# Attention and two expert layers on one core: another order of the first transfers, other places for the steps of the heads, and two of three blocks of the first chunk among the last heads

## The chip, the core and the metric

The kernel runs on one core of a Trainium2 chip. Its engines work side by side, each through its own queue in order: TensorE (PE; its weight loads are PEld), VectorE (DVE), ScalarE (ACT), GpSimd (POOL) and SyncE (SP), which issues all the DMAs. The metric is the device time of one execution in microseconds.

## The reference

```python
q_assign = argmax(q_n @ c_n)            # per head, 16 normalised centroids
k_assign = argmax(k_n @ c_n)
mask = q_assign[:, :, :, None] == k_assign[:, :, None, :]
scores = where(mask, scale * q @ k.T, -1e9); attn = softmax(scores) @ v   # 2 x 8 heads, 768 x 64
x = attn.transpose(0, 2, 1, 3).reshape(1536, 512)
p = domain_probs / (domain_probs.sum(-1) + 1e-9)
out = sum over 4 experts e of p[:, e] * (relu(x @ w1[e]) @ w2[e])     # 512 -> 1024 -> 512
h = out @ w_in; result = maximum(0.01 * h, h) @ w_out                 # 512 -> 2048 -> 512
```

## The kernel before

The sixteen (batch, head) pairs are heads t = 0 to 15; two make a pair `pr`. For each head the kernel needs a stack of q and k halves (`qka`, `qkb`), made from `pair` by three DMAs (`restack`), and two small DMAs that add the one-hot cluster rows (`restack_oh`). Pieces of a head:

- `M(t,j)`, j = 0 to 5: scores of 128 rows on PE, their row maximum by DVE (L416). `mrow(t)`: PE transposes the six maxima, ACT copies them, a DMA writes them into `qka`; E of that head needs it.
- `E(t,s)`: scores on PE (L447, L448), exponential on ACT into one of three `p` buffers. `P(t,s)`: `phi` and the rest `plo`, in float16. POOL makes `plo`, but in heads 14 and 15 DVE does.
- `V(t,j)`: 18 small products (L473 to L475) that read `phi` and `plo` of all six s. `norm(t)`: division on DVE. `X(pr)`: PE transposes a finished pair, ACT and DVE split it into `xhi` and `xlo`, the input of the first expert layer.
- For a coming pair: `prep_load` of q, k, v; `prep_T` (transposes of q, k); `prep_simT`, `sims_argmax`, three argmax pieces and `prep_ohT` (the cluster rows); `prep_vmax`, `prep_vall`, `prep_vscale` and `prep_v` (v scaled and split).

PE results go through three double banks `big()` in turn, V through two single ones. All steps stand in one list (`at(when, ...)`), sorted by a hand-written place: `E(t,s)` has place 6t + s, and constants such as `M_AT`, `V_AT`, `MROW_AT` and `RESTACK_AT` give the others relative to a head or a pair. Each engine takes its part of the steps in that order, SP its DMAs too. So a DMA that must wait holds up all DMAs behind it.

At the start the SP order is: q, k of pairs 0 and 1; restack(0); v of pair 0; restack(1); v of pair 1; the small `dp`; the one-hot rows of head 1; restack(2), restack(3); q, k of pair 2; the one-hot rows of heads 2 and 3; q, k of pair 3.

`open_early` (place 78.5) closes the pool `prep` and loads the first weights `w1raw` and the probabilities `pb`; `split_early` (84.5) splits these weights (ACT, POOL) and loads the next ones into the same `w1raw`.

The expert layers run in 16 and then 8 chunks of 256 hidden columns: hidden products for three blocks u of 512 tokens, an epilogue (DVE `g`, ACT `hhi`, POOL `hlo`), then twelve output tiles. Of chunk 0, block u = 0 (24 products, L637) is put among the last steps: 12 before the last head's V, 6 behind them, 6 behind X(7); its epilogue `h_finish` is one DVE instruction over two banks (L656). The pools `main` and `psum_a` are then closed, `ffn` and `psum_f` opened over the same memory, and blocks 1 and 2 follow (L872). `input_sums` are 18 steps for the later seven-product chunks, spread by `quota` over chunks 0 and 1.

Of the kernel before, what the change touches and what calls it, by code (L numbers as in the profile page):

```python
# [8 lines left out]
F32 = mybir.dt.float32  # L9
# [5 lines left out]
ALU = mybir.AluOpType  # L15
# [3 lines left out]
PHI_AT = 0.97  # L19
PHI_ON_VECTOR = ((0, 2, 5), (3,))  # L20
PLO_ON_VECTOR = ((), ())
M_AT = ((0.72, 1.85, 2.02, 3.21, 4.53, 5.24), (0.67, 1.71, 2.17, 2.76, 4.15, 5.08))
V_AT = ((1.8, 2.31, 3.68, 4.42, 5.11, 5.44), (1.09, 2.97, 3.59, 4.57, 5.82, 5.87))
NORM_AT = (6.53, 6.37)
PREP_V_AT = (2.42, 2.77)
MROW_AT = (-0.08, 1.32)
X_AT = 4.26
VMAX_AT = 3.85
VSCALE_AT = 7.41
T_AT = (3.21, 3.57)  # L30
SIMT_AT = 5.56
SIMS_AT = 6.98
ARGMAX_AT = (1.05, 2.1, 2.22)
OHT_AT = 3.04
RESTACK_AT = (0.42, 1.63)


M0_AT = (-6.63, -3.55, -2.57, -2.19, -1.41, -1.01)
# [8 lines left out]
PHI_FIRST = ((1, 2), (3, 5))  # L47
WARM = (7, 2, 6)
WARM_AT = (4.39,)

BIG = float(2 ** 60)
HEAD_ROOM = 64.0
# [7 lines left out]
def attention_moe_kernel(  # L60
# [13 lines left out]
    nc = tc.nc  # L74
    B, H, S, D = q.shape
# [7 lines left out]
    J = S // 128  # L83
# [22 lines left out]
    def big():  # L106
        pool, tag = bigs[turns[0] % len(bigs)]
        turns[0] += 1
        return pool.tile([128, 1024], F32, tag=tag, name=tag)
# [25 lines left out]
    def h_set(pool):  # L135
        n = len(hbuf)
        hbuf.append([pool.tile([128, FCH // 128, NT], F32R, name=f"h{x}{n}") for x in ("hi", "lo")])
        gbuf.append(pool.tile([128, FCH // 128, 512], F32, name=f"g{n}"))
        pbuf.append(pool.tile([128, 1, NT], F32, name=f"pb{n}"))
# [47 lines left out]
    def split_halves(hi, lo, src):  # L187

        nc.scalar.activation(out=hi, in_=src, func=AF.Copy)  # L189
        n = src.shape[1] // 2  # L190
        for x in (slice(0, n), slice(n, 2 * n)):
            nc.gpsimd.tensor_tensor(out=lo[:, x], in0=src[:, x], in1=hi.bitcast(F32)[:, x], op=ALU.subtract)  # L192

    def weights_split(part):
        hi, lo = (w1s, w2s)[part][0]
        split_halves(hi, lo, raw12[part])

    def weights_sums():

# [372 lines left out]
    prep_T(0, 0)  # L572
    prep_T(0, 1)
    restack(0)
    prep_load(0, "v")
    restack(1)
    prep_load(1, "v")
    dp = prep.tile([128, NTILE, E], F32, name="dp")
    nc.sync.dma_start(
        out=dp.rearrange("p (b j) e -> p b (j e)", b=B),  # L580
# [40 lines left out]
    NF = FCH // 128  # L621
    h_ps = {}

    def h_products(c, u, n0, n1):

        if n0 == 0:
            h_ps[c, u] = big()
        pv = h_ps[c, u].rearrange("p (f t) -> p f t", f=NF)
        whi, wlo = w1s[0]
        us = slice(u * 512, (u + 1) * 512)  # L630
        n = 0
        for f in range(NF):
            fs = slice(f * 128, (f + 1) * 128)
            for kc in range(KC):
                for i, (w, x) in enumerate(((whi, xhi), (whi, xlo), (wlo, xhi))):
                    if n0 <= n < n1:
                        nc.tensor.matmul(  # L637
                            pv[:, f, :], lhsT=w[:, kc, fs], rhs=x[:, kc, us],
                            start=kc + i == 0, stop=kc == KC - 1 and i == 2,
                        )  # L640
                    n += 1
# [21 lines left out]
            nc.vector.tensor_tensor(out=g, in0=src, in1=g, op=ALU.max)  # L663
        split(hi, lo, g, nc.gpsimd)

    def h_finish(c, u):
        h_split(c, u, 0, h_ps.pop((c, u)).rearrange("p (f t) -> p f t", f=NF))

    NMM = 3 * NF * KC

    def open_early():
        st_prep.close()
        early = ctx.enter_context(tc.tile_pool(name="early", bufs=1, side="right"))
        w1_set(early)
        raw12.append(early.tile([128, KC, FCH], F32, name="w1raw"))
        h_set(early)
        weights_load(0, 0)
        probs_load(0)

    def split_early():  # L680
        weights_split(0)
# [5 lines left out]
    def at(when, fn, *args):  # L687
        line.append((when, len(line), fn, args))

    for t in range(NH):  # L690
        o = J * t
        par = t % 2
        for s in range(J):
            at(o + s, emit_E, t, s)
            if t < NH - 2:
                at(o + s + PHI_AT, emit_P, t, s, s in (PHI_ON_VECTOR[par] if t > 1 else PHI_FIRST[t]), s in PLO_ON_VECTOR[par])
            else:
                at(o + s + PHI_AT, emit_P, t, s, s % 2 == 0, True)
        for j in range(J):
            if t > 1:  # L700
                at(o - 2 * J + M_AT[par][j] if t > 3 else (M2_AT, M3_AT)[t - 2][j], emit_M, t, j)
            at(o + J + V_AT[par][j], emit_V, t, j)
        at(o + J + NORM_AT[par], emit_norm, t)
        at(o + PREP_V_AT[par] if t > 0 else EARLY["v0"], prep_v, t)
        if t > 1:
            at(o - J + MROW_AT[par] if t > 3 else EARLY[f"mrow{t}"], emit_mrow, t)
# [34 lines left out]
    at(EARLY["ohT0"] + 0.01, restack_oh, 1)  # L741
    for t in (2, 3):
        at(EARLY["restack"], restack, t)
    for nm in "qk":
        at(EARLY["restack"] + 0.01, prep_load, 2, nm)
    for t in (2, 3):
        at(EARLY["ohT1"] + 0.01, restack_oh, t)
    at(EARLY["vmax"], prep_vmax, 0)
# [4 lines left out]
    for when in WARM_AT:  # L753
        at(when, warm, 1)
    at(J * (NH - 3) + 0.5, open_early)
    at(J * (NH - 2) + 0.5, split_early)

    end = J * NH + V_AT[(NH - 1) % 2][0]
    at(end - 0.01, h_products, 0, 0, 0, NMM // 2)
    end = J * NH + NORM_AT[(NH - 1) % 2]  # L760
    at(end + 0.01, h_products, 0, 0, NMM // 2, 3 * NMM // 4)
    at(J * (NH + 1) + X_AT + 0.01, h_products, 0, 0, 3 * NMM // 4, NMM)
    at(J * (NH + 1) + X_AT + 0.02, h_finish, 0, 0)
    for _, _, fn, args in sorted(line, key=lambda x: x[:2]):
        fn(*args)
    st_main.close()
# [2 lines left out]
    ffn = ctx.enter_context(tc.tile_pool(name="ffn", bufs=1))  # L769
    psum_f = ctx.enter_context(tc.tile_pool(name="psum_f", bufs=1, space=bass.MemoryType.PSUM))  # L770
    w2_set(ffn)
    raw12.append(ffn.tile([128, FCH // 128, DM], F32, name="w2raw"))
    gbuf.append(ffn.tile([128, FCH // 128, 512], F32, name="g1"))
    pbuf.append(ffn.tile([128, 1, NT], F32, name="pb1"))
    acc = ffn.tile([128, NTILE * DM], F32, name="acc")
# [192 lines left out]
    def is_wide(c):  # L968
        return wide and chunks[c][3] is None

    weights_load(0, 1)
    probs_load(1)
    turns[1] = 0
    PLAIN = (0, 1, N1, N1 + 1)
# [1 line left out]
    for c in range(NCH):  # L976

        steps = []
        if c + 1 < NCH and is_wide(c + 1):
            steps += weights_narrow(c + 1, 0)  # L980
            if c + 2 < NCH:
                steps.append(lambda: weights_load(c + 2, 0))
        if c + 1 < NCH and not is_wide(c + 1):
            steps.append(lambda: weights_load(c + 1, 1))
        if c in PLAIN:
            weights_split(1)
            if c == 0:
                sums_left = input_sums(False)
                quota = [5, 5, 5, 5]
            n = quota.pop(0)  # L990
            slots = steps + sums_left[:n]
            sums_left = sums_left[n:]
            blocks = [(u, f) for u in range(1 if c == 0 else 0, NU) for f in range(NF)]
            for n, (u, f) in enumerate(blocks):
                if c > 0:
                    ps = bank(BANKS[u][f])
                    plain(c, u, f, ps)
                elif f == 0:
                    both_ps = [bank(BANKS[u][f]) for f in range(NF)]
                    for k in range(KC):  # L1000
                        for g in range(NF):
                            plain(c, u, g, both_ps[g], [k])
                if c == 0:
                    ps = both_ps[f]
                h_split(c, u, f, ps)
                for _ in range(-(-len(slots) // (len(blocks) - n))):
                    step = slots.pop(0)
                    if step:
                        step()
        else:  # L1010
            emit_seven(c, steps)

        steps, later = [], []
        if c in PLAIN:
            n = quota.pop(0)
            later, sums_left = sums_left[:n], sums_left[n:]
        if c + 1 < NCH:
            if is_wide(c + 1):
                later += weights_narrow(c + 1, 1)
                if c + 2 < NCH:  # L1020
                    later.append(lambda: weights_load(c + 2, 1))
            steps.append(lambda: weights_split(0))
            if c + 1 not in PLAIN:
                steps += weights_sums()
            if c + 2 < NCH and not is_wide(c + 2):
                steps.append(lambda: weights_load(c + 2, 0))
        if c == N1 - 5 and wide:
            steps += [lambda: weights_load(N1, 0), lambda: weights_load(N1, 1)]
        if c < N1 and c % (FE // FCH) == 0 and 0 < chunks[c][3] < E - 1:
            steps.append(lambda: probs_load(chunks[c][3] + 1))  # L1030
        steps = [x for pair in zip_longest(steps, later) for x in pair if x]
        for i in range(NTILE):
            if c == N1 - 1 and i == NTILE - 1:
                sums_left = input_sums(True)
                quota = [3, 2, 4, 4]
                sums_left.pop(0)()
            (emit_y1 if c < N1 else emit_y2)(c, i)
            for _ in range(-(-len(steps) // (NTILE - i))):
                steps.pop(0)()
# [32 lines left out]
```

## Time and profile before

| | us |
|---|---|
| three runs, median | 1045.18 (1044.88 to 1045.35) |
| profiled execution | 1047.64 |
| its span, first to last instruction | 1045.9 |
| PE busy in the span | 1012.0 (97%) |
| DVE, POOL, ACT busy | 674.9, 602.2, 400.9 |
| mean granted TensorE clock | 0.992 |

PE is busy in nearly all of the span; a queue of matmuls counts as busy, at full clock or at half. What the chip does otherwise with its time shows where PE waits or where its clock is down.

### The profile page before, as it was taken

The numbers are of one execution on the slowest core, as the hardware profiler recorded it, in microseconds if no ns is written. First come the engines' busy times: TensorE is split into PE (matmuls) and PEld (weight loads), VectorE is DVE, ScalarE is ACT, GpSimd is POOL, SyncE is SP. The second block draws the span as 40 slices with busy tenths as digits, with TensorE's granted clock in tenths as the row PEclk, the third lists the DMA queues.
The fourth block names the chain that finished last, engine by engine and source line by source line (L and its number), as shares of the span: only waits on it lengthen the run. The fifth ranks groups of instructions, "written<-read, shape, count | busy, mean of one in ns | idle before, by whom it ended". The sixth has DMA issues, their size and how long they took to land.

```text
span 1045.9 us, 15196 instructions
## 1 busy us (share of the span) xinstructions
PE 1012.0 (97%) x6064; PEld 824.5 (79%) x6064; DVE 674.9 (65%) x964; ACT 400.9 (38%) x554; POOL 602.2 (58%) x468
## 2 busy tenths in 40 slices
PE   7689999999999999999999999999999999999998
PEld 5578888878788888888888888888877888888886
DVE  7698888887754454444544445544587678777765
ACT  3467777775321222212122222222245433344331
POOL 4267777781645566545665455654577565665553
PEclk9899999999999999999999999999999999999999
DMA  7854666540310110210111103101111221122103
GB/s 174 171 111 109 137 146 145 115 102 21 72 40 21 41 41 24 68 36 25 40 52 40 41 21 121 41 21 41 40 41 41 81 81 43 45 74 81 41 1 121
DMA packets 59535, 70.74 MB, mean 68 GB/s; under 512 B 25060, under 2 KB 42088, under 8 KB 59464
## 3 DMA queue, kind: packets, MB, share of 16 engines
q1 hardware_dynamic: 59464, 69.77, 25.4%
q8 instruction: 48, 0.79, 0.3%
q14 instruction: 23, 0.19, 0.1%
HBM read 46.19 MB, written 3.17 MB: 47 GB/s over the span
## 4 chain that ended last, share of the span: by engine, by line
PE 70%; DVE 3%; ACT 1%; issue 0%; POOL 0%; DVEq 0%; POOLq 0%
PE z L862 18%; PE z L872 15%; PE z L939 8%; PE z L938 8%; PE z L937 8%; PE z L955 4%; PE z L957 4%; PE z L956 4%; ACT xhi L119 0%; DVE xlo L120 0%; DVE acc L944 0%; DVE g L663 0%; POOL hlo L120 0%; DVE w2raw L173 0%; DVE w2raw L182 0%
## 5 line engine op out<-in xcount | busy, mean ns | idle before, releaser
L120 POOL TENSOR_TENSOR hlo<-g,hhi 128x512 fp32r<-128x512 f32 (+1 forms) x143 | 198.5, 1396 | 293.7 <-ACT hhi L119 292.3
L944 DVE TENSOR_TENSOR acc<-z,acc 128x512 f32<-128x512 f32 x180 | 124.0, 690 | 101.5 <-PE z L939 101.4
L461 POOL TENSOR_TENSOR plo<-p,phi 128x768 f16<-128x768 f32 x84 | 138.1, 1656 | 85.2 <-ACT phi L460 47.0
L119 ACT ACTIVATE hhi<-g 128x512 fp32r<-128x512 f32 (+1 forms) x143 | 89.5, 635 | 189.7 <-DVE g L656 143.9
L939 PE MATMUL z<-hlo,w2hi 128*128 128x512 f32 x384 | 152.9, 398 | 0.0
L938 PE MATMUL z<-hhi,w2lo 128*128 128x512 f32 x384 | 151.6, 395 | 0.0
L937 PE MATMUL z<-hhi,w2hi 128*128 128x512 f32 x384 | 150.9, 393 | 0.4 <-DVE acc L944 0.4
L656 DVE SCALAR_TENSOR_TENSOR g<-z,pb 128x512 f32<-128x512 f32 x80 | 55.0, 688 | 92.5 <-PE z L872 86.5
L872 PE MATMUL z<-xhi,w1hi 128*128 128x512 f32 x248 | 98.2, 396 | 1.7 <-DVE g L656 1.7
L872 PE MATMUL z<-xlo,w1hi 128*128 128x512 f32 x248 | 98.4, 397 | 0.0
L872 PE MATMUL z<-xhi,w1lo 128*128 128x512 f32 x248 | 98.2, 396 | 0.0
L416 DVE TENSOR_REDUCE m<-big 128x1 f32<-128x768 f32 x96 | 90.2, 949 | 12.1 <-PE big L412 10.8
L450 ACT ACTIVATE p<-big 128x768 f32<-128x768 f32 x96 | 77.8, 810 | 37.4 <-PE big L448 34.0
L938 PEld LDWEIGHTS z<-hhi,w2lo 128*128 128x128 f32 x384 | 72.1, 188 | 18.3
L937 PEld LDWEIGHTS z<-hhi,w2hi 128*128 128x128 f32 x384 | 72.1, 188 | 18.1 <-DVE acc L944 0.8
L939 PEld LDWEIGHTS z<-hlo,w2hi 128*128 128x128 f32 x384 | 72.1, 188 | 16.8
L955 PE MATMUL z<-w2hi,hhi 128*128 128x512 f32 x192 | 76.7, 400 | 2.2 <-DVE acc L960 2.2
L447 PE MATMUL big<-qka 128*128 128x512 f32 x192 | 73.2, 382 | 4.0 <-DMA qka<-mrow 2.1
L956 PE MATMUL z<-w2lo,hhi 128*128 128x512 f32 x192 | 76.8, 400 | 0.0
L957 PE MATMUL z<-w2hi,hlo 128*128 128x512 f32 x192 | 76.8, 400 | 0.0
L895 DVE TENSOR_TENSOR part<-z,part 128x512 f32<-128x512 f32 x60 | 41.5, 692 | 52.3 <-PE z L862 42.2
L192 POOL TENSOR_TENSOR w2lo<-w2raw,w2hi 128x512 fp32r<-128x512 f32 x48 | 61.2, 1298 | 22.9 <-ACT w2hi L189 22.9
(196 smaller groups left out, 2291.6 us busy)
## 6 DMA issues: line engine op xcount, KB each, us to landing
qkb<-pair SPq DMA_DIRECT2D x32, 384.0 KB, 6.8
w1raw<-in_moe_w_dram SPq DMA_DIRECT2D x16, 512.0 KB, 3.5
w2raw<-in_moe_w_dram SPq DMA_DIRECT2D x16, 512.0 KB, 3.6
w1raw<-in_moe_w_in_dram SPq DMA_DIRECT2D x8, 1024.0 KB, 7.1
w2raw<-in_moe_w_out_dram SPq DMA_DIRECT2D x8, 1024.0 KB, 5.0
qka<-pair SPq DMA_DIRECT2D x16, 384.0 KB, 4.0
vraw<-in_v_dram SPq DMA_DIRECT2D x16, 192.0 KB, 3.0
pb<-pe_rows SPq DMA_DIRECT2D x4, 768.0 KB, 8.0
```

Of the source, the lines that this page charges most:

```text
L120: lo_engine.tensor_tensor(out=lo, in0=src, in1=hi.bitcast(F32), op=ALU.subtract)
L416: nc.vector.tensor_reduce(out=m_t[t][:, j:j + 1], in_=ps[:, 0:S], op=ALU.max, axis=AX.X)
L461: (nc.vector if plo_on_vector else nc.gpsimd).tensor_tensor(out=plo, in0=p, in1=phi, op=ALU.subtract)
L862: nc.tensor.matmul(ps[:, 0, :], lhsT=w[i][:, k, :], rhs=x[j][:, k, :], start=first and k + i + j == 0, stop=k == 1 and i == 1, skip_group_ ...
L872: nc.tensor.matmul(ps[:, 0, :], lhsT=w[:, k, fs], rhs=x[:, k, us], start=k + i == 0, stop=k == KC - 1 and i == 2,)
L937: nc.tensor.matmul(ps, lhsT=whi[:, f, ks], rhs=hi[:, f, us], start=f == 0, stop=False)
L938: nc.tensor.matmul(ps, lhsT=wlo[:, f, ks], rhs=hi[:, f, us], start=False, stop=False)
L939: nc.tensor.matmul(ps, lhsT=whi[:, f, ks], rhs=lo[:, f, us], start=False, stop=f == NF - 1)
L944: nc.vector.tensor_tensor(out=a, in0=ps, in1=a, op=ALU.add)
L955: nc.tensor.matmul(ps, lhsT=hi[:, f, ts], rhs=whi[:, f, :], start=f == 0, stop=False)
L956: nc.tensor.matmul(ps, lhsT=hi[:, f, ts], rhs=wlo[:, f, :], start=False, stop=False)
L957: nc.tensor.matmul(ps, lhsT=lo[:, f, ts], rhs=whi[:, f, :], start=False, stop=f == NF - 1)
```

## The change

Most step places of the steady heads, the order of the first transfers, the place of the second weights' loads, and the place and epilogue of the first chunk's blocks 0 and 1 are other ones; the last two heads get V and norm places of their own. The DMAs at the start now go: restack(0), restack(1), q and k of pair 2, `dp`, one-hot rows of head 1, v of pair 0, restack(2), restack(3), v of pair 1, one-hot rows of heads 2 and 3. `w2raw` is loaded in `open_early`, behind `w1raw` and `pb`. Block 0 is finished before X(7) but for its epilogue; block 1 has six products before X(7) and eighteen behind it; the epilogues are single-bank instructions whose `g` lies in the `p` buffers. `w2lo` of chunk 0 is made by one DVE instruction in place of two on POOL.

```diff
-M_AT = ((0.72, 1.85, 2.02, 3.21, 4.53, 5.24), (0.67, 1.71, 2.17, 2.76, 4.15, 5.08))
-V_AT = ((1.8, 2.31, 3.68, 4.42, 5.11, 5.44), (1.09, 2.97, 3.59, 4.57, 5.82, 5.87))
-NORM_AT = (6.53, 6.37)
-MROW_AT = (-0.08, 1.32)
+M_AT = ((1.25, 2.08, 2.35, 3.21, 5.26, 5.79), (0.67, 1.9, 2.06, 2.76, 4.04, 5.42))
+V_AT = ((1.84, 2.15, 2.31, 3.56, 4.97, 5.13), (1.44, 2.97, 3.24, 4.31, 4.57, 5.82))
+NORM_AT = (6.53, 6.12)
+MROW_AT = (1.43, 0.25)
...
-VSCALE_AT = 7.41
+VSCALE_AT = 9.19
...
-SIMS_AT = 6.98
-ARGMAX_AT = (1.05, 2.1, 2.22)
-OHT_AT = 3.04
-RESTACK_AT = (0.42, 1.63)
+SIMS_AT = 6.7
+ARGMAX_AT = (1.36, 2.0, 2.3)
+OHT_AT = 3.0
+RESTACK_AT = (-0.21, 1.47)
...
+V_LAST = ((1.23, 2.31, 4.28, 5.08, 5.75, 5.98), (1.09, 1.44, 1.57, 4.46, 5.87, 5.87))
+NORM_LAST = (6.49, 6.57)
+PHI_LAST = ((0, 2, 4), (0, 2, 4))
+SPLIT_AT = (0.94,)
+FILL = ((0, 0, 1.07), (0, 6, 1.08), (0, 12, 6.38), (0, 18, 6.39), (1, 0, 9.94), (1, 6, 10.27), (1, 12, 10.27))
...
     restack(0)
-    prep_load(0, "v")
     restack(1)
-    prep_load(1, "v")
+    prep_load(2, "qk")
...
+    def h_finish_early(u):
+        hi, lo = [x[:, :, u * 512:(u + 1) * 512] for x in hbuf[0]]
+        pv = h_ps.pop((0, u)).rearrange("p (f t) -> p f t", f=NF)
+        for f in range(NF):
+            g = main.tile([128, S], F32, tag="p", name="p", bufs=3)[:, 0:512]
+            nc.vector.scalar_tensor_tensor(
+                out=g, in0=pv[:, f, :], scalar=0.0, in1=pbuf[0][:, 0, u * 512:(u + 1) * 512], op0=ALU.max, op1=ALU.mult,
+            )
+            split(hi[:, f, :], lo[:, f, :], g, nc.gpsimd)
...
         weights_load(0, 0)
         probs_load(0)
+        weights_load(0, 1)
...
-    for nm in "qk":
-        at(EARLY["restack"] + 0.01, prep_load, 2, nm)
+    at(EARLY["ohT0"] + 0.02, prep_load, 0, "v")
+    at(EARLY["restack"] + 0.01, prep_load, 1, "v")
...
-    at(J * (NH - 2) + 0.5, split_early)
+    at(J * (NH - 2) + SPLIT_AT[0], split_early)
...
+    for u, n, when in FILL:
+        at(J * NH + when, h_products, 0, u, n, n + 6)
+    end = J * (NH + 1) + X_AT
+    at(end + 0.02, h_finish_early, 0)
+    at(end + 0.04, h_products, 0, 1, 18, NMM)
+    at(end + 0.05, h_finish_early, 1)
...
-            weights_split(1)
+            weights_split(1, nc.vector if c == 0 else None)
             if c == 0:
                 sums_left = input_sums(False)
-                quota = [5, 5, 5, 5]
+                quota = [0, 6, 6, 6]
```

## Rows read from the trace of the kernel before

**Rows 1.** Windows: busy time by engine in three stretches, then clock, DMA share, GB/s.
```profile
60.00:215.00 155.00, 148.99 (x1899) 129.32 (x1898) 138.19 (x210) 120.50 (x164) 109.96 (x67) 1.00 0.57 123
215.00:265.20 50.20, 44.23 (x638) 38.55 (x635) 38.80 (x58) 31.77 (x44) 20.50 (x13) 0.97 0.27 69
...
293.30:1045.90 752.60, 745.86 (x3193) 600.79 (x3191) 435.18 (x596) 216.17 (x305) 432.86 (x357) 1.00 0.15 48
```

**Rows 2.** Waits of PE, 60 to 215 us, the largest: in total, times, longest.
```profile
PE big L326 <- DVE oh L306: 1.8, 5, 0.4
```

**Rows 3.** Waits of PE, 215 to 266 us.
```profile
PE big L447 <- DMA qka<-mrow: 2.1, 1, 2.1
PE z L872 <- DVE g L656: 1.7, 1, 1.7
PE big L412 <- DMA qka<-ohT: 1.2, 1, 1.2
PE big L412 <- DVE m L416: 0.8, 1, 0.8
```

**Rows 4.** Timeline of PE at the start; in brackets idle time and what ended it.
```profile
29.50 0.59 PE L412 MATMUL big<-qka 96*128 96x512 f32 x2 [2.67 <-DMA qka<-ohT]
...
43.48 1.52 PE L255 MATMUL big<-ident,qraw 128*128 128x128 f32 x6 [4.99 <-DMA qraw<-in_q_dram]
...
48.69 0.54 PE L412 MATMUL big<-qka 96*128 96x512 f32 x2
```

**Rows 5.** Timeline of SP's DMA issues at the start: start, length, what.
```profile
13.88 4.14 SPq L244 DMA_DIRECT2D vraw<-in_v_dram  x2
...
25.65 1.97 SPq L361 DMA_DIRECT2D qka<-ohT  x2
...
36.62 3.69 SPq L244 DMA_DIRECT2D qraw<-in_q_dram  x2
...
41.91 2.67 SPq L361 DMA_DIRECT2D qka<-ohT  x4
```

**Rows 6.** Window of two microseconds at the start, columns as in group 1.
```profile
42.00:44.00 2.00, 0.52 (x3) 0.55 (x4) 0.00 (x0) 0.00 (x0) 0.00 (x0) 0.50 1.15 235
```

**Rows 7.** Timeline of PE in the last heads: E(14,0), E(14,1), E(15,0), V(14,0).
```profile
232.82 0.47 PE L447 MATMUL big<-qka 128*128 128x512 f32 x1
...
233.60 0.40 PE L447 MATMUL big<-qka 128*128 128x512 f32 x1
...
243.38 0.76 PE L447 MATMUL big<-qka 128*128 128x512 f32 x1 [2.11 <-DMA qka<-mrow]
...
246.08 0.28 PE L473 MATMUL small<-vt,phi 128*128 128x65 f16 x1
```

**Rows 8.** The page's costliest groups: count, busy us, mean ns, idle before.
```profile
L120 POOL TENSOR_TENSOR hlo<-g,hhi 128x512 fp32r<-128x512 f32 (+1 forms) x143 | 198.5, 1396 | 293.7 <-ACT hhi L119 292.3
...
L656 DVE SCALAR_TENSOR_TENSOR g<-z,pb 128x512 f32<-128x512 f32 x80 | 55.0, 688 | 92.5 <-PE z L872 86.5
...
L416 DVE TENSOR_REDUCE m<-big 128x1 f32<-128x768 f32 x96 | 90.2, 949 | 12.1 <-PE big L412 10.8
```

**Rows 9.** Timeline of SP's DMA issues in the last heads.
```profile
211.49 0.75 SPq L434 DMA_DIRECT2D qka<-mrow  x1
...
221.83 0.40 SPq L163 DMA_DIRECT2D w1raw<-in_moe_w_dram  x1
...
239.59 0.37 SPq L163 DMA_DIRECT2D w1raw<-in_moe_w_dram  x1
240.00 0.75 SPq L434 DMA_DIRECT2D qka<-mrow  x1
```

**Rows 10.** Timeline of DVE in the last heads.
```profile
238.43 1.55 DVE L399 SCALAR_TENSOR_TENSOR vt<-vraw,vsc,vt 128x384 f16<-128x384 f32 x1
...
242.82 1.83 DVE L461 TENSOR_TENSOR plo<-p,phi 128x768 f16<-128x768 f32 x2
```

**Rows 11.** Timeline of DVE: the epilogue of block 0.
```profile
263.75 1.22 DVE L656 SCALAR_TENSOR_TENSOR g<-big,pb 128x1024 f32<-128x1024 f32 x1
```

More of the change, by code (lines that the diff above doesn't have):

```diff
@@ L21 @@
 PLO_ON_VECTOR = ((), ())
-M_AT = ((0.72, 1.85, 2.02, 3.21, 4.53, 5.24), (0.67, 1.71, 2.17, 2.76, 4.15, 5.08))
-V_AT = ((1.8, 2.31, 3.68, 4.42, 5.11, 5.44), (1.09, 2.97, 3.59, 4.57, 5.82, 5.87))
-NORM_AT = (6.53, 6.37)
-PREP_V_AT = (2.42, 2.77)
-MROW_AT = (-0.08, 1.32)
+M_AT = ((1.25, 2.08, 2.35, 3.21, 5.26, 5.79), (0.67, 1.9, 2.06, 2.76, 4.04, 5.42))
+V_AT = ((1.84, 2.15, 2.31, 3.56, 4.97, 5.13), (1.44, 2.97, 3.24, 4.31, 4.57, 5.82))
+NORM_AT = (6.53, 6.12)
+PREP_V_AT = (2.41, 2.77)
+MROW_AT = (1.43, 0.25)
 X_AT = 4.26
-VMAX_AT = 3.85
-VSCALE_AT = 7.41
+VMAX_AT = 3.98
+VSCALE_AT = 9.19
 T_AT = (3.21, 3.57)
-SIMT_AT = 5.56
-SIMS_AT = 6.98
-ARGMAX_AT = (1.05, 2.1, 2.22)
-OHT_AT = 3.04
-RESTACK_AT = (0.42, 1.63)
+SIMT_AT = 5.6
+SIMS_AT = 6.7
+ARGMAX_AT = (1.36, 2.0, 2.3)
+OHT_AT = 3.0
+RESTACK_AT = (-0.21, 1.47)
 M0_AT = (-6.63, -3.55, -2.57, -2.19, -1.41, -1.01)
@@ L192, in split_halves, with weights_split @@
             nc.gpsimd.tensor_tensor(out=lo[:, x], in0=src[:, x], in1=hi.bitcast(F32)[:, x], op=ALU.subtract)
-    def weights_split(part):
+    def weights_split(part, lo_engine=None):
         hi, lo = (w1s, w2s)[part][0]
-        split_halves(hi, lo, raw12[part])
+        if lo_engine:
+            split(hi, lo, raw12[part], lo_engine)
+        else:
+            split_halves(hi, lo, raw12[part])
     def weights_sums():
@@ L622, in attention_moe_kernel @@
     h_ps = {}
+    born = {}
     def h_products(c, u, n0, n1):
@@ L627, in h_products @@
             h_ps[c, u] = big()
+            born[c, u] = turns[0]
+        assert turns[0] - born[c, u] < 3 or c > 0 or u > 1
         pv = h_ps[c, u].rearrange("p (f t) -> p f t", f=NF)
-        whi, wlo = w1s[0]
+        whi, wlo = w1s[c % 2]
         us = slice(u * 512, (u + 1) * 512)
         n = 0
-        for f in range(NF):
-            fs = slice(f * 128, (f + 1) * 128)
-            for kc in range(KC):
+        for kc in range(KC):
+            for f in range(NF):
+                fs = slice(f * 128, (f + 1) * 128)
                 for i, (w, x) in enumerate(((whi, xhi), (whi, xlo), (wlo, xhi))):
@@ L664, in h_split @@
         split(hi, lo, g, nc.gpsimd)
-    def h_finish(c, u):
-        h_split(c, u, 0, h_ps.pop((c, u)).rearrange("p (f t) -> p f t", f=NF))
     NMM = 3 * NF * KC
+    def h_finish_early(u):
+        hi, lo = [x[:, :, u * 512:(u + 1) * 512] for x in hbuf[0]]
+        assert turns[0] - born[0, u] < 3
+        pv = h_ps.pop((0, u)).rearrange("p (f t) -> p f t", f=NF)
+        for f in range(NF):
+            g = main.tile([128, S], F32, tag="p", name="p", bufs=3)[:, 0:512]
[3 more added lines that the diff above has]
+            split(hi[:, f, :], lo[:, f, :], g, nc.gpsimd)
     def open_early():
@@ L675, in open_early @@
         raw12.append(early.tile([128, KC, FCH], F32, name="w1raw"))
+        raw12.append(early.tile([128, FCH // 128, DM], F32, name="w2raw"))
         h_set(early)
@@ L697, in attention_moe_kernel @@
             else:
-                at(o + s + PHI_AT, emit_P, t, s, s % 2 == 0, True)
+                at(o + s + PHI_AT, emit_P, t, s, s in PHI_LAST[par], True)
         for j in range(J):
@@ L701, in attention_moe_kernel @@
                 at(o - 2 * J + M_AT[par][j] if t > 3 else (M2_AT, M3_AT)[t - 2][j], emit_M, t, j)
-            at(o + J + V_AT[par][j], emit_V, t, j)
-        at(o + J + NORM_AT[par], emit_norm, t)
+            at(o + J + (V_AT if t < NH - 2 else V_LAST)[par][j], emit_V, t, j)
+        at(o + J + (NORM_AT if t < NH - 2 else NORM_LAST)[par], emit_norm, t)
         at(o + PREP_V_AT[par] if t > 0 else EARLY["v0"], prep_v, t)
@@ L755, in attention_moe_kernel @@
     at(J * (NH - 3) + 0.5, open_early)
-    at(J * (NH - 2) + 0.5, split_early)
[L758 to L763, printed above, removed]
+    at(J * (NH - 2) + SPLIT_AT[0], split_early)
[5 more added lines that the diff above has]
+    at(end + 0.05, h_finish_early, 1)
     for _, _, fn, args in sorted(line, key=lambda x: x[:2]):
@@ L771, in attention_moe_kernel @@
     w2_set(ffn)
-    raw12.append(ffn.tile([128, FCH // 128, DM], F32, name="w2raw"))
     gbuf.append(ffn.tile([128, FCH // 128, 512], F32, name="g1"))
@@ L969, in is_wide @@
         return wide and chunks[c][3] is None
-    weights_load(0, 1)
     probs_load(1)
@@ L992, in attention_moe_kernel @@
             sums_left = sums_left[n:]
-            blocks = [(u, f) for u in range(1 if c == 0 else 0, NU) for f in range(NF)]
+            blocks = [(u, f) for u in range(2 if c == 0 else 0, NU) for f in range(NF)]
             for n, (u, f) in enumerate(blocks):
```

## The prediction

> **What bounds the kernel now.** First the windows by stretch, to see where TensorE is full. From 293 us on it is busy 745.9 of 752.6 us [rows 1]; the change touches only the placing of a few DVE steps there. From 60 to 215 us 155.0 - 149.0 = 6.0 us are idle, from 215 to 265 us another 6.0, and there the mean clock is 0.97, which is 0.03 x 50.2 = 1.5 us of clock. Then the waits of PE by stretch, to see what ends them: in the steady heads the largest is for the one-hot result of DVE, five times, 1.8 us in all [rows 2]; in the last heads it is a DMA of the maxima row, 2.1 us, then the hand-over to the expert layers, the one-hot DMA of head 15 and a maximum of DVE [rows 3]. At the start the timeline of PE shows two stops for DMAs, 2.67 and 4.99 us [rows 4]. So there are three places for a gain, some 8, 6 and 7 us deep; the rest is full. All DMAs go through SP in order, so the timeline of SP tells why a DMA came late [rows 5, 9].
>
> **The start.** The 4.99 us stop is T(2,0) waiting for q of pair 2, which SP issued at 36.62 behind four restacks and both v loads [rows 4, 5]. The change issues it before the one-hot rows of head 1, and v of pair 0 behind them. The bytes ahead of those rows are the same (q and k of a pair are four loads of 192 KB, v of two pairs too), so the first stop, for head 1, stays; I take it as unchanged, with up to 1 us more since the v loads hold SP for 4.14 us a pair and the q and k loads for about as much [rows 5]. T(2,0), E(0,3), T(2,1) and E(0,4) then run under what was the second stop. What is late next is M(2,0), the step behind them: it needs the one-hot rows of head 2, and ahead of those the same set of transfers stands as before, only permuted. They were issued at 41.91; head 1's were issued at 25.65 and let PE go at 29.50, 3.85 us later [rows 4, 5]. So M(2,0) can start at 41.91 + 3.85 = 45.8 and not at 48.69: 2.9 us won, not 4.99, and the stop moves there at some 4 us.
>
> At 42 to 44 us the granted clock is 0.50, the 1.2 GHz level [rows 6], after PE had stood idle from 38.5; the four steps from 43.48 to 48.69 take 5.21 us. E at full clock takes 233.60 - 232.82 = 0.78 us; from 243.38, also at the low level, two take 246.08 - 243.38 = 2.70, 1.35 each [rows 7]. So a stop of this length costs 0 (its dip falls on idle time) to 5.21 x (1 - 0.78/1.35) = 2.2 us of work behind it. In the new place that work is DVE-paced in part, so I take 1.0. Start: 2.9 - 1.0 = 1.9, between 0 (dip whole, head 1 a microsecond later) and 5.0 (the one-hot rows come in time). The Trainium skill's page TensorE: Matmul & The Clock Gate, section What's actually happening, says an idle array is put at half clock and comes back only behind sustained work; by it the full 2.2 would be paid and the start gives 0.7. Rows 6 and 7 show both levels, but not which stop is long enough.
>
> **The steady heads.** Won: V(.,2) of even heads moves from behind the one-hot transposes (places 9.68 and 9.04) to before them (8.31 and 9.0), while the argmax pieces keep their order on DVE; the wait there, at most 0.4, is shorter than one E of 0.78, and a V of 18 products goes in front of it. I take all 1.8 [rows 2, 7]. The other 4.2 us are waits for banks and `plo`; `prep_vscale` leaves the place where it delayed a maximum, and I take 0.5. Lost: M(odd,5) goes from 5.08 to 5.42 and mrow(odd) from 1.32 to 0.25 of the next head. Between them PE now has one E of 0.78, and DVE needs 0.95 for the maximum [rows 7, 8]; PE stands in order behind the transposes, with the next E and M queued behind. At least 0.17 a head, I take 0.25, for t = 5, 7, ..., 15: 6 x 0.25 = 1.5. Steady: 1.8 + 0.5 - 1.5 = 0.8, between -6 and +6.
>
> **The last heads.** Five terms.
> (a) restack(15) stood on SP behind mrow(13), issued at 211.49 [rows 9]. mrow(13) is one E, one M and one V earlier now, more than the 1.2 us that M(15,0) waited for the one-hot rows [rows 3]: 1.1, between 0 and 1.2.
> (b) The maxima row of head 15 was issued at 240.00, right behind the second `w1raw`, which SP held until 239.59 for the split of the first [rows 9]. mrow(15) now stands at 84.25, `split_early` at 84.94, so the row is in SP before the load. The 2.1 us stop of E(15,0) goes and, with it, the half-clocked stretch: up to 2.1 + 1.5 = 3.6. What is late next is DVE: V(14,0) needs the last `plo` of head 14, done at 242.82 + 1.83 = 244.65, and stood at 246.08 [rows 7, 10], so 1.4 if DVE is no earlier. I take 2.2, as `prep_vscale` now fills an idle place of DVE.
> (c) The 0.8 us wait for a maximum: between 0 and 0.8, I take 0.3.
> (d) Hand-over: the first `z` product waited 1.7 us for the epilogue's 1.22 us on DVE [rows 3, 11]. Both blocks' epilogues now precede it; block 0's pieces are hidden under 18 products of block 1, block 1's two take 2 x 0.69 = 1.38 [rows 8]: -0.2. The `w2` tiles lie in `ffn` over the `p` buffers, so ACT's `w2hi` waits for four POOL subtractions of 1.4 each [rows 8], behind it the next `hhi`; block 2's 24 products cover this just about: 0 to -1.4, I take -0.3. The Trainium skill's page SBUF — State Buffer, section SBUF: two separate sides, says that a DVE instruction with two SBUF inputs and a POOL one exclude each other; the `vt` step of 1.55 us at 238.43 stands beside POOL's split [rows 10] and agrees, and by that rule `w2lo` on DVE could lose another POOL operation, so -1.7 in place of -0.3.
> (e) mrow(14) goes from 77.92 to 79.43, behind `open_early`, so its DMA queues behind `w1raw`, `pb` and now `w2raw`: 0.51 + 0.77 + 0.51 = 1.8 MB from 221.83 - 1.5 = 220.3 on. At 235 GB/s [rows 6] that ends at 228, at the 123 GB/s of the steady heads [rows 1] at 235. E(14,0) needs it at 232.82 - 1.5 = 231.3 [rows 7]. Between 0 and -3.7, I take -0.2.
> Moved products of blocks 0 and 1 are the same ones at the same price: nothing. Last heads: 1.1 + 2.2 + 0.3 - 0.2 - 0.3 - 0.2 = 2.9.
>
> **Sum.** 1.9 + 0.8 + 2.9 = 5.6 us. The profiled execution of 1047.64 (span 1045.9 and 1.7 around it) becomes 1042.0; the runs' median is 2.46 below it, so 1039.6.
>
> **Rivals.** *Every stop simply goes.* Nothing takes the place of the stops: 5.0 at the start, 2.3 in the steady heads, 1.2 + 3.6 + 0.8 less 0.7 in the last: 12.2, time 1033.0. For it speaks that PE is full wherever it has data; against it the named next waits, M(2,0) and `plo`, both seen in the rows.
> *The stops come back.* The weights' three loads go at the slower rate, E(14,0) stops 3.7 us, M(2,0) pays its clock dip (0.7 for the start) and the V(14,0) bound holds (1.4): 0.7 + 0.8 + 1.1 + 1.4 + 0.3 - 0.2 - 0.3 - 3.7 = 0.1, time 1045.1. Three pieces each possible alone; a share of them gives 1043 to 1045.
> *The odd maxima rows pace PE.* At mrow(odd) DVE may have `xlo` and another maximum of 0.95 each ahead of the one needed: 3 x 0.95 - 0.78 = 2.07 a head, 12.4 in six heads, against gains of 5.6 + 1.5 = 7.1: time 1045.18 - 7.1 + 12.4 = 1050.5. It turns slower than before by 2.1 us from (7.1 + 2.1)/6 = 1.5 a head. DVE is busy 138.2 of 155 us [rows 1], which speaks for a queue there; that nothing but this maximum is placed for DVE just before it speaks against.
>
> **Numbers.** A run of this kernel can tell about 0.2%, 2.1 us, from no change. Forecast (1036.5 to 1043.0) 0.57; every stop goes 0.12; the stops come back 0.19; odd rows 0.08, and 0.04 for E(14,0) later still. So faster 0.69, same 0.19, slower 0.12. The range from 1034.5 to 1046.0 leaves out most of the slower cases and the lower half of the first rival; the forecast's own is 1036.5 to 1043.0.
>
> **What the changed profile would show.** Start: no wait for `qraw`, a wait of about 4 us for `qka<-ohT` at M(2,0), at some 46 us. Steady: no wait of L326 for `oh`, a new one of L431 for `m`, under 0.4 each. Last heads: no wait for `mrow`, none for head 15's one-hot rows, a wait of L475 for `plo` under 1 us, L872 waiting 1.9 us, y products starting without a wait. The prediction is wrong if M(2,0) does not wait, if L431 waits over a microsecond, or if E(14,0) waits for its row.

## The result and the profile after

The changed kernel takes 1037.03 us, median of 4 runs (1034.72 to 1038.70), beside 1045.26 for the kernel before: a ratio of 0.9914, 95% interval 0.9895 to 0.9934. It is faster, by 8.2 us where 5.6 were forecast. A second set of 6 runs gave 1036.66 beside 1045.57, ratio 0.9908 (0.9890 to 0.9926). The profiled execution took 1036.60 with a span of 1034.9, so between the two profiles, this one and the one of [rows 1], there are 11.0 us.

To see where they lie, the same four instructions are looked up in each trace: the last E of head 1, the first E of head 12, the first `y` product and the last product (of that one its end). Between them stand the start, the steady heads, the last heads with the hand-over, and the full rest.

```
us from the span's start   E(1,5)   E(12,0)  first y  last    | start  steady  last heads  rest
before                     68.24    208.32   276.42   1041.80 | 68.24  140.08  68.10       765.38
after                      64.82    200.47   265.39   1030.77 | 64.82  135.65  64.92       765.38
after, second profile      67.20    202.85   267.75   1031.55 | 67.20  135.65  64.90       763.80
```

So the steady heads gave 4.4 us, the last heads 3.2, both to 0.02 us alike in two profiles. The start gave 3.4 in one profile and 1.0 in the other.

Windows by stretch of the changed kernel, columns as in [rows 1]: the first heads, the steady heads, the last heads.
```profile
29.97:37.80 7.83, 7.83 (x30) 6.81 (x31) 4.45 (x8) 1.98 (x4) 0.00 (x0) 0.50 0.95 228
...
60.00:215.00 155.00, 150.49 (x1930) 132.37 (x1929) 137.13 (x214) 120.37 (x165) 114.62 (x70) 1.00 0.59 132
215.00:259.70 44.70, 41.75 (x559) 36.04 (x559) 33.85 (x52) 27.33 (x40) 16.46 (x12) 1.00 0.16 47
```
From 215 to 260 us the clock is full (0.97 before, [rows 1]); at the start 7.83 us of work run at 0.50, behind the first stop.

Timeline of its PE at the start, M(1,0) and M(2,0), answering [rows 4]:
```profile
29.97 0.98 PE L422 MATMUL big<-qka 96*128 96x512 f32 x2 [4.51 <-DMA qka<-ohT]
...
45.18 0.58 PE L422 MATMUL big<-qka 96*128 96x512 f32 x2 [0.34 <-DMA qka<-ohT]
```
Timeline of SP, the issues of their one-hot rows, answering [rows 5]:
```profile
27.03 1.24 SPq L371 DMA_DIRECT2D qka<-ohT  x2
...
42.08 2.47 SPq L371 DMA_DIRECT2D qka<-ohT  x4
```
The stop for q is gone. The one-hot rows of heads 1 and 2 are issued when they were before, within 1.4 and 0.2 us [rows 5]; M(2,0) starts at 45.18 and not at 48.69 [rows 4]. M(1,0) starts 0.47 later than before.

Waits of its PE, 60 to 215 us, the largest (before: [rows 2]); these are the transposes of the odd maxima rows, and `r` is the norm's first step, which VectorE does right behind the maximum:
```profile
PE big L441 <- DVE r L496: 2.2, 5, 0.4
```
Waits of its PE, 215 to 260 us, all that are shown (before: [rows 3]):
```profile
PE z L896 <- DVE p L688: 1.5, 1, 1.5
PE small L485 <- DVE plo L471: 1.0, 2, 0.6
PE small L485 <- POOL plo L471: 0.8, 1, 0.8
```
The four waits of [rows 3] are gone but the hand-over's, which fell from 1.7 to 1.5. In the place of the rows' DMAs stand V steps that wait for `plo`, and VectorE's timeline shows it working on these without a break (before: [rows 10]):
```profile
231.97 1.83 DVE L471 TENSOR_TENSOR plo<-p,phi 128x768 f16<-128x768 f32 x2
233.72 0.55 DVE L468 CAST phi<-p 128x768 f16<-128x768 f32 x1
234.30 1.83 DVE L471 TENSOR_TENSOR plo<-p,phi 128x768 f16<-128x768 f32 x2
```

### The profile page after: what moved, and what is told of

Same layout as the page of the kernel before. It is cut to its first block, busy times and chain, and to the rows that moved or that the text cites. A ratio compares the mean times of both kernels' runs of the same rounds, so it can differ in the third digit from the quotient of the medians.

```text
span 1034.9 us, 15188 instructions
## 1 busy us (share of the span) xinstructions
PE 1008.1 (97%) x6064; PEld 822.4 (79%) x6064; DVE 672.4 (65%) x966; ACT 398.2 (38%) x555; POOL 597.4 (58%) x467
## 4 chain that ended last, share of the span: by engine, by line
PE 87%; DVE 8%; SPq 2%; ACT 2%; issue 1%; POOL 0%; DMA 0%; DVEq 0%; ACTq 0%; POOLq 0%
PE z L886 19%; PE z L896 15%; PE z L963 8%; PE z L962 8%; PE z L961 8%; PE z L979 4%; PE z L981 4%; PE z L980 4%; PE big L422 3%; PE big L457 3%; PE big L458 2%; DVE m L426 2%; PE small L483 1%; PE small L484 1%; PE small L485 1%; PE big L650 1%
## 5 line engine op out<-in xcount | busy, mean ns | idle before, releaser
L127 POOL TENSOR_TENSOR hlo<-g,hhi 128x512 fp32r<-128x512 f32 x140 | 191.8, 1379 | 266.6 <-ACT hhi L126 265.2
L126 ACT ACTIVATE hhi<-g 128x512 fp32r<-128x512 f32 x140 | 87.2, 632 | 178.7 <-DVE g L669 132.8
L896 PE MATMUL z<-xhi,w1hi 128*128 128x512 f32 x240 | 95.0, 396 | 1.5 <-DVE p L688 1.5
L896 PE MATMUL z<-xlo,w1hi 128*128 128x512 f32 x240 | 95.3, 397 | 0.0
L896 PE MATMUL z<-xhi,w1lo 128*128 128x512 f32 x240 | 95.0, 396 | 0.0
L199 POOL TENSOR_TENSOR w2lo<-w2raw,w2hi 128x512 fp32r<-128x512 f32 x46 | 58.7, 1299 | 25.9 <-ACT w2hi L196 25.9
```

The costliest lines, as they stand in the source:

```text
L127: lo_engine.tensor_tensor(out=lo, in0=src, in1=hi.bitcast(F32), op=ALU.subtract)
L896: nc.tensor.matmul(ps[:, 0, :], lhsT=w[:, k, fs], rhs=x[:, k, us], start=k + i == 0, stop=k == KC - 1 and i == 2,)
```

## The experiments

**The three parts alone.** Each was put into the kernel before: the order of the first transfers, the steady places, the last heads with the hand-over; and in the changed kernel the odd maxima rows were moved behind one more E.

Start alone (a_start):
```diff
     restack(0)
-    prep_load(0, "v")
     restack(1)
-    prep_load(1, "v")
+    prep_load(2, "qk")
...
-    for nm in "qk":
-        at(EARLY["restack"] + 0.01, prep_load, 2, nm)
+    at(EARLY["ohT0"] + 0.02, prep_load, 0, "v")
+    at(EARLY["restack"] + 0.01, prep_load, 1, "v")
```


> The kernel before with the new order of the first transfers alone (q and k of pair 2 ahead of the one-hot rows of head 1, both v loads behind them). By the prediction's term 1.9 us faster, 1043.4, with a stop of about 4 us at M(2,0). By the lead that the changed profile shows at the end of head 1 (3.4 us; M(2,0) waits 0.34 us, because TensorE comes to it late after a 4.51 us stop at head 1 and 10.2 us at the low clock) 1041.9, and the same short wait. Rival: the 2.4 us by which the profiled execution of before lay above its median were lost at the start, and the order itself gives 1.0 or less: 1044.3.

Measured: 1043.24 beside 1046.46, ratio 0.9967 (0.9952 to 0.9982), by the ratio 3.5 us faster, between 1.9 and 5.0. PE's timeline shows the two stops of the changed kernel again:
```profile
29.89 0.98 PE L412 MATMUL big<-qka 96*128 96x512 f32 x2 [4.47 <-DMA qka<-ohT]
...
45.03 0.58 PE L412 MATMUL big<-qka 96*128 96x512 f32 x2 [0.20 <-DMA qka<-ohT]
```
M(2,0) waits shortly, as the second theory had it; the gain is nearest to it, and its interval just reaches the prediction's 1.9.

Steady places alone (c_steady; heads 14 and 15 keep the old tables, here `V_END`, `NORM_END`, `MROW_END`):
```diff
-M_AT = ((0.72, 1.85, 2.02, 3.21, 4.53, 5.24), (0.67, 1.71, 2.17, 2.76, 4.15, 5.08))
+M_AT = ((1.25, 2.08, 2.35, 3.21, 5.26, 5.79), (0.67, 1.9, 2.06, 2.76, 4.04, 5.42))
...
-VSCALE_AT = 7.41
+VSCALE_AT = 9.19
...
-        at(o + J + V_AT[par][j], emit_V, t, j)
+        at(o + J + (V_AT if t < NH - 2 else V_END)[par][j], emit_V, t, j)
```


> The kernel before with the new places of the steady heads alone (heads 14 and 15 keep their V steps, norms and maxima rows, split and hand-over). The places alone move the one-hot rows of head 15 ahead too. By the prediction's terms 0.8 + 1.1 = 1.9 us faster, 1043.4. By the lead of the changed profile, which grows by 3.9 us from head 1 to head 13, 3.9 + 1.1 = 5.0: 1040.3, with no wait of the maxima or one-hot transposes but the odd maxima row's 0.4 each. Rival: with the old start and end the places give back part at the last heads (the row of head 15 is still behind the second load of w1), so that under 1 us remains: 1044.5.

Measured: 1039.29 beside 1046.46, ratio 0.9935 (0.9923 to 0.9947): by the ratio 6.8 us, more than any theory said. In its trace the steady heads take 135.73 us (4.4 less than before) and the last heads 66.00 (2.1 less), though nothing of the last heads was edited but what the M steps' and restacks' places bring. (The profile gains 2.0 more at the start and near 790 us, where the low clock fell otherwise.) The three largest waits of its PE in the last heads:
```profile
PE z L877 <- DVE g L661: 1.7, 1, 1.7
PE big L436 <- DVE m L421: 1.1, 1, 1.1
PE big L452 <- DMA qka<-mrow: 0.8, 1, 0.8
```
The one-hot wait of head 15 is gone, and the maxima row, still behind the second load of `w1`, costs 0.8 and not 2.1 [rows 3]; no stretch there runs at the low clock.

Last heads and hand-over alone (b2_tail; the changed kernel with the old start and the old tables; heads 14 and 15 keep the new V places, norms and maxima rows, and the products of blocks 0 and 1 keep their new order, `for kc` outside `for f`, which no run has alone):
```diff
-M_AT = ((1.25, 2.08, 2.35, 3.21, 5.26, 5.79), (0.67, 1.9, 2.06, 2.76, 4.04, 5.42))
+M_AT = ((0.72, 1.85, 2.02, 3.21, 4.53, 5.24), (0.67, 1.71, 2.17, 2.76, 4.15, 5.08))
+MROW_END = (1.43, 0.25)
...
-            at(o - J + MROW_AT[par] if t > 3 else EARLY[f"mrow{t}"], emit_mrow, t)
+            at(o - J + (MROW_AT if t < NH - 2 else MROW_END)[par] if t > 3 else EARLY[f"mrow{t}"], emit_mrow, t)
```


> The kernel before with the new last heads and hand-over alone (maxima rows of heads 14 and 15, split, V steps and norms of heads 14 and 15, block 1 among them, both blocks finished early, the w2 load early, w2lo on DVE); start and steady heads as before. By the prediction's terms without (a) 1.8 us faster, 1043.5. By the lead of the changed profile, 3.7 us from head 13 to the first y product less (a) 1.1 = 2.6: 1042.7. The waits for the row of head 15 and the dip of the clock behind it are gone, the one-hot wait of head 15 (1.2) stays. Rival: all of the stop and its dip come back as gain, 3.6 us and more: 1041.6 or less.

Measured: 1046.10 beside 1046.46, ratio 0.9997 (0.9986 to 1.0008): no gain. Its last heads take 67.46 us, 0.6 less than before. The two largest waits of its PE there, and a window:
```profile
PE big L425 <- DMA qka<-ohT: 1.6, 1, 1.6
PE small L488 <- DVE plo L474: 1.3, 2, 0.7
```
```profile
222.40:226.00 3.60, 3.60 (x43) 3.06 (x42) 1.21 (x2) 2.23 (x4) 2.67 (x2) 0.69 0.81 229
```
The row's stop of 2.1 and its half-clocked stretch are gone, but the stop for the one-hot rows of head 15 grew from 1.2 [rows 3] to 1.6, and now it has a stretch at the low clock behind it (0.69 in the window); V then waits 1.3 for `plo`. The stall moved one step ahead. The parts of the new end were not tested one by one.

Odd maxima rows behind one more E (d_odd):
```diff
-            at(o - J + MROW_AT[par] if t > 3 else EARLY[f"mrow{t}"], emit_mrow, t)
+            at(o - J + (1.1 if par and t < NH - 1 else MROW_AT[par]) if t > 3 else EARLY[f"mrow{t}"], emit_mrow, t)
```


> The changed kernel with the maxima rows of the odd heads 5 to 13 behind the second E of the head before (place 1.1 instead of 0.25; head 15 keeps 0.25). If the 0.44 us that the transposes wait in each of the five pairs is the price of standing one E behind their maximum, it is won back: 5 x 0.44 = 2.2, 1034.8, and the pair shrinks from 26.85 to 26.4 us. Rival: VectorE paces the stretch and the next M or E waits for a bank in its place: 1036.6 to 1037.0, the pair stays at 26.85.

Measured: 1036.45, ratio 0.9906 (0.9892 to 0.9920), and four pairs, from the start of head 4 to that of head 12, take 107.38 us where the changed kernel takes 107.37. The windows of this stretch, first of the changed kernel, then of this one:
```profile
93.10:200.47 107.37, 105.33 (x1346) 93.19 (x1345) 95.26 (x148) 84.39 (x117) 78.79 (x49) 1.00 0.61 134
```
```profile
93.06:200.44 107.38, 106.20 (x1346) 93.14 (x1345) 95.27 (x148) 83.73 (x117) 78.80 (x49) 1.00 0.62 134
```
The named waits of 0.44 are gone, PE counts as busy 0.9 longer, and the time is the same. The chain of work that ended last tells why. Behind one M step of a pair (start, length, what) it runs so in the changed kernel:
```profile
146.99 0.96 DVE m L426
147.95 0.14 DVE r L496
148.09 0.27 PE big L441
...
150.98 0.41 PE big L422
```
and so in this one:
```profile
146.96 0.96 DVE m L426
147.91 0.14 DVE r L496
...
148.31 0.56 DVE xn L500
148.86 1.06 DVE phi L468
149.93 0.88 DVE m L426
...
150.85 0.50 PE big L422
```
In the changed kernel the chain leaves VectorE behind the 0.44 stop and follows TensorE to the next M. With the stop gone it stays on VectorE for 3.9 us: a maximum, the norm's three steps, a `phi`, the next maximum, and only then may M go on. From the first maximum to that M it is 3.99 us with the stop and 3.89 without: of the 0.44 VectorE's string leaves 0.1 here, and over the four pairs nothing.

**Within the steady places.** Four kernels, each measured once, and the stretch from E(4,0) to E(12,0):

The third V of even heads alone, in the kernel before:
```diff
-V_AT = ((1.8, 2.31, 3.68, 4.42, 5.11, 5.44), ...
+V_AT = ((1.8, 2.31, 2.31, 4.42, 5.11, 5.44), ...
```


> The kernel before with the third V step of the even heads alone moved, from behind the one-hot transposes to before them (place 2.31 instead of 3.68). The prediction took for it the whole wait of the transposes, 0.36 us a pair: from the start of head 4 to that of head 12, 109.94 us before, 108.5. Rival: the gain is given back at the V steps' old place, where the wait for a maximum grows: 109.9. For comparison, all steady places together: 107.44.

All steady places but those of M, and the places of M alone in the kernel before (the `M_AT` line of the diff above, undone and done):

> The kernel with the steady places alone (as in c_steady), but the M steps back where they were before. Those waits of M and E for a maximum that the new places removed (0.33 and 0.15 us a pair) return if the M places took them away: heads 4 to 12 in 107.44 + 1.9 = 109.3. If the moved V steps and prep_vscale freed the banks, the stretch stays at 107.4 to 107.8. The prediction's 0.5 us for banks allows 0.4 at most.

> The kernel before with the new places of the M steps of the steady heads alone. Heads 4 to 12 took 109.94 us before, 107.44 with all places, 111.0 with all but these, 109.93 with the one V step alone. If the M places are what wins, 107.5 to 108; if M, V and the row places only fit together, 109.5 or more.

All steady places but that of `prep_vscale` (`VSCALE_AT = 7.41`):

> The kernel with the steady places alone (as in c_steady), but prep_vscale back at its old place. The prediction gave it most of its 0.5 us for banks and plo, 0.1 a pair: heads 4 to 12 in 107.8. If prep_vscale delays a maximum that M waits for (0.33 us a pair before), 108.8. If it costs nothing where it stood, 107.4.

Measured, with the stretch ahead of it, heads 2 and 3, beside it:
```
                                    E(1,5) to E(4,0)   E(4,0) to E(12,0)   PE waits named in the latter
before                              30.13 us           109.94 us           3.0 us
V(.,2) alone                        30.13              109.93              2.2
M places alone                      30.48              110.79              3.0
all but the M places                29.39              111.01              4.2
all but prep_vscale                 29.40              107.45              none
all (old start, old end)            28.29              107.44              1.8
changed kernel                      28.28              107.37              1.8
changed, odd rows one E later       28.29              107.38              none
```
Waits of PE from E(4,0) to E(12,0), V(.,2) alone:
```profile
PE big L412 <- DVE m L416: 1.2, 4, 0.3
PE big L447 <- DVE m L416: 1.0, 5, 0.2
```
all but the M places:
```profile
PE big L417 <- DVE eq L308: 1.9, 4, 0.5
```
and, from E(1,5) to E(4,0), all but `prep_vscale`:
```profile
PE small L480 <- POOL plo L466: 0.8, 1, 0.8
```
With the one V step moved the one-hot wait of [rows 2] is gone, and the waits of M and E for a maximum grow from 1.6 to 2.2 us: nothing is won. The M places alone lose 0.9. All but the M places lose 1.1, through a single stop for one-hot rows: the pair that has it takes 28.6 us, the three others 27.5 each, which is the 27.5 of before, so without it 0.1 is won at most. Together they win 2.5. `prep_vscale` costs nothing where it stood in these four pairs, but 1.1 us once, in heads 2 and 3. There its steps stand on VectorE ahead of a `phi`, which starts at 71.10, 3.04 us behind E(1,5), and not 1.90 behind it as with all places; POOL's `plo` comes later by as much, and a V waits for it (0.9 us before, 0.8 here, not at all with all places).

What the places took away shows in the chain. That of the kernel before does not pass through these heads, but that of the version with the new last heads alone does, and its steady heads are the old ones (140.05 us beside 140.08). Of its 109.9 us from E(4,0) to E(12,0) 62.6 lie on TensorE, 36.3 on VectorE and 5.3 on ScalarE; in the changed kernel 102.6 of 107.4 lie on TensorE and 4.4 on VectorE. The longest of the old strings, once in each pair, are the one-hot pieces with maxima between them, 4.8 us up to the one-hot transposes:
```profile
169.06 0.57 DVE mx L315
...
170.25 0.93 DVE eq L317
171.18 0.87 DVE m L429
172.04 0.46 DVE mb L318
172.50 0.47 DVE m L429
...
173.29 0.55 DVE oh L319
```
The wait named at its end is 0.4 us [rows 2].

**Does the new end pay on top of the rest?** New start and steady places, old last heads and hand-over (ac_start_steady):
```diff
+V_END = ((1.8, 2.31, 3.68, 4.42, 5.11, 5.44), (1.09, 2.97, 3.59, 4.57, 5.82, 5.87))
+MROW_END = (-0.08, 1.32)
...
     restack(1)
-    prep_load(1, "v")
+    prep_load(2, "qk")
```


> The kernel before with the new start and the new steady places, and the old last heads and hand-over. If the parts add, 3.5 + 6.8 = 10.3 us faster than before, and the changed kernel's last heads are worth nothing or cost 1 to 2 us. By the prediction's terms (b) to (e), 1.8 us, it is 1.8 slower than the changed kernel (ratio to before 0.993). By the trace: from head 13 to the first y product the lead grew 2.8 us with the steady places alone and 3.75 in the changed kernel, so the new end is worth 1.0 (ratio 0.9924).

Measured: 1036.37 beside 1046.19, ratio 0.9905 (0.9889 to 0.9921), as fast as the changed kernel. In its trace the last heads take 66.23 us, 1.3 more than the changed kernel's; the medians can't show 1.3. The one execution that was profiled was its slowest, 1042.26 (the other five lie between 1036.15 and 1036.74): the low clock fell on 8 to 15 us as well, and E(1,5) came at 68.96.

The changed kernel again:

> The changed kernel once more, for a second profile and a second interval beside the version without its last heads. Ratio 0.9914 as before, within 0.002. If the two profiles differ by more than a microsecond, the traces place it: at the start (before head 1 ends) or at the stop behind the first weight halves near 790 us, where the low clock came in some profiles and not in others.

Measured as given above. The profiles differ by 2.38 us at E(1,5), and by 1.6 the other way later (last section). At the start, M(1,0) and M(2,0), and the window of the second stop:
```profile
30.26 0.58 PE L422 MATMUL big<-qka 96*128 96x512 f32 x2 [1.97 <-DMA qka<-ohT]
...
45.79 0.76 PE L422 MATMUL big<-qka 96*128 96x512 f32 x1 [2.03 <-DMA qka<-ohT]
```
```profile
43.70:52.20 8.50, 6.47 (x23) 5.04 (x23) 4.73 (x9) 3.75 (x6) 4.54 (x3) 0.60 0.59 138
```
M(2,0) starts at 45.18 in the first profile and 45.79 in this one, but here 6.8 us at the low clock lie behind it.

**A faster start?** In the changed kernel (x1) the rows of head 1 were put ahead of q and k of pair 2, and v of pair 1 behind the rows of heads 2 and 3; then (best) the same start with the steady places, the old end, and only the row of head 15 ahead of the load:
```diff
     restack(1)
-    prep_load(2, "qk")
...
-    at(EARLY["ohT0"] + 0.02, prep_load, 0, "v")
-    at(EARLY["restack"] + 0.01, prep_load, 1, "v")
+    at(EARLY["ohT0"] + 0.015, prep_load, 2, "qk")
+    at(EARLY["ohT0"] + 0.02, prep_load, 0, "v")
+    at(EARLY["ohT1"] + 0.02, prep_load, 1, "v")
```


> The changed kernel with the one-hot rows of head 1 ahead of q and k of pair 2, and v of pair 1 behind the one-hot rows of heads 2 and 3. If the 4.51 us stop at head 1 comes from the bytes that stand ahead of its rows on SP, it goes to under 1 us, and the dip of the clock behind it with it, up to 3 us more; what is late next is M(2,0), whose rows come 3.6 us earlier with v out of the way. So 3 to 6 us faster than the changed kernel, ratio 0.986 to 0.9885. Rival: the same bytes land at the same rate and M(2,0) waits where M(1,0) did: under 1 us gained, ratio 0.991.

Measured: 1036.08, ratio 0.9903 (0.9886 to 0.9919). In PE's timeline M(1,0) starts at 27.31, behind a stop of 1.89, and M(2,0) at 43.61, behind one of 1.68. The first rows come 2.7 us earlier, the second 1.6, and both are waited for; the median moves by less than it can tell, and the 3 to 6 us did not come.

> New start and steady places, the old last heads and hand-over with two things alone: the maxima row of head 15 ahead of the second load of w1 (place 0.25, split at 0.94), and the start's one-hot rows of head 1 ahead of q and k of pair 2, v of pair 1 behind those of heads 2 and 3. The wait for the row of head 15 (1.0 us without it) goes: if nothing takes its place, 1.0 faster than without, and 0.65 more from the start as the trace of x1 showed: ratio 0.989. If VectorE's plo takes the place of the row, as in the changed kernel (1.04 us of waits there), no more than the start's 0.65: 0.990. Rival: the changed kernel's whole end is needed, and this is slower than it: 0.9925.

Measured: 1038.07, ratio 0.9914 (0.9892 to 0.9935), so no better. Its M(1,0) waits 0.39 us, and its M(2,0), which starts at 45.45, waits 6.08. The row of head 15 is not waited for, and the last heads take 65.49 us: 0.7 less than with the old end, 0.6 more than with the whole new one. No version beat the changed kernel by more than the runs can tell.

## Why the prediction was right, and where its terms were not

**Direction and size.** Faster was right, 5.6 forecast, 8.2 and 8.9 measured; the time lies in the forecast's own range, near its low end. That it does is in part luck: the steady heads gave 3.6 us more than their term, in a way that the sum did not have.

**The start, 1.9.** The step "M(2,0) can start at 41.91 + 3.85 = 45.8" holds: 45.18 and 45.79 in the changed kernel, 45.03 with the start alone. (In the slowest profile, of new start and steady places, it was 47.51, its rows issued 0.7 us later and 4.7 on the way.) "The stop moves there at some 4 us" does not: 0.34 and 2.03, because TensorE itself comes there only at 44.84 and 43.76. The half-clocked stretch was expected to cost 1.0; in one profile it lay behind the first stop and took 7.83 us of work, in the other 6.8 us of it lay behind M(2,0). Because M(2,0) is bound by its rows, slow work ahead of it costs nothing and slow work behind it counts: 3.4 with the one, 1.0 with the other, a median of 3.5 (1.9 to 5.0) alone. The bounds 0 to 5.0 held. That the Trainium skill's page TensorE: Matmul & The Clock Gate, section What's actually happening, lets an idle array fall to half clock agrees with these windows; the price worked out from it, 0.7 for the start in all, is what came nearest in the second profile (1.0), not in the first.

**The steady heads, 0.8: the step that failed.** Measured 4.4: 1.85 in heads 2 and 3, 2.57 in the four pairs behind them. The term was a sum of waits, "I take all 1.8", "I take 0.5", "6 x 0.25 = 1.5", and the waits were no prices. The one-hot wait taken away alone gave 0.01. The new wait of the odd rows, 0.44 as named and not 0.25, could be taken away without a gain (107.38 for 107.37). `prep_vscale` was mis-sized: 1.1 in heads 2 and 3, with the rest of the new places in, and nothing in the four pairs. Waits of 0 to 1.8 us stand beside the same 107.4 us. What won 2.5 in the four pairs is the places of M with those of the other steps; alone the M places lost 0.9, and the others, their one stop for rows taken off, won 0.1 at most. What the sum missed is the path: with the old places the chain lay on VectorE for 36.3 of 109.9 us, with the new ones for 4.4 of 107.4, so TensorE now holds the pair itself. VectorE's busy time doesn't tell this: it is 97.6 us there before and 95.3 after, and 93.9 with the M places alone, which is slower than before. Which single move takes which string off the path was not tested.

**The last heads, 2.9.** Measured 3.2, with the waits gone that (a), (b) and (c) named, and `plo` as (b)'s next late thing: 1.0 us of DVE's in two pieces, where "under 1 us" was said, and 0.8 of POOL's. (d) put 1.9 for the hand-over, 1.5 was measured, and `y` started without a wait. VectorE's share of `w2` fell where POOL stood idle (263.36 to 264.59 us), so the loss that (d) names by the port rule of the Trainium skill's page SBUF — State Buffer, section SBUF: two separate sides, had no case there. In the steady heads the trace agrees with that rule: of the `vt` steps, two inputs each, the one at 126.42 us, where POOL's `plo` ends, takes 0.61 us, and the one at 142.01, beside a `plo` that ends at 143.01, takes 1.42. (e), E(14,0) waiting for its row, did not come. But (b) was not the new end's to win: the steady places alone took 2.1 of the 3.2 (the row's stop fell to 0.8, without a dip), and the end alone 0.6, since head 15's one-hot rows then stopped TensorE for 1.6 us, with the low clock behind the stop. The new end is worth 1.1 to 1.3 on top of the rest by the traces, and is not seen in the medians.

**The rivals.** "The odd maxima rows pace PE" had the wrong price: the rows' wait is 0.44 and costs nothing. VectorE's string holds that piece of the pair only when the rows stand later, at the same pair of 26.85 us. "Every stop simply goes", 12.2 us, is near what lay between the two profiles (11.0), though stops stayed; 2.5 of that is how far the profile of before lay above its runs. "The stops come back" was right of the start in so far as each rearrangement handed its wait to the next rows; its 0.7 is near the 1.0 of the second profile only.

## What to carry to other kernels

A wait that the profile names is not a price. Before counting it, ask what the engine would wait for next; time the repeating stretch between the same two instructions, compare kernels by that, and follow the chain to see whose work fills it. Where two engines feed each other in turn, move their steps together: one half of a good new order may be slower than the old one, or win nothing. At the start each transfer put ahead on SP here passed the wait on to the next rows.

Look up the same few instructions in both traces before explaining a difference: here a third of the difference between two profiles came from a start that varied by 2.4 us in one kernel.

## What was not expected of the chip

The same stop was followed by the low clock in one execution and not in the next. Near 790 us TensorE stops for 2.26 us in one profile of the changed kernel and for 2.24 in the other; the 4.5 us of work behind it, in the windows of the one and of the other:
```profile
791.10:795.60 4.50, 4.50 (x13) 3.55 (x14) 3.41 (x5) 2.51 (x3) 4.50 (x4) 0.62 0.01 2
```
```profile
793.40:797.90 4.50, 4.46 (x19) 3.67 (x20) 3.42 (x5) 2.52 (x3) 4.50 (x4) 1.00 0.00 2
```
13 products against 19, and 1.6 us over the rest of the span (765.38 against 763.80). Of the fourteen profiles ten have the low clock behind this stop. So neither a stop's length nor the code decides alone; a price of 0 to 1.6 us for it is a range and not an estimate to be split.
